# Loads of w_in for two chunks at once, an order of their own for the weight loads, and a shifted attention of batch 1

One core of one Trainium2 chip. The metric is the device time of the whole kernel in microseconds (us), lower is better.

## The reference

```python
# 8 batches, 8 heads, 576 rows, 64 columns a head; 4608 tokens, 512 model columns, 2048 hidden columns
kv = np.einsum('bhsd,bhse->bhde', k, v)
out = np.einsum('bhsd,bhde->bhse', q, kv)
rms = np.sqrt(np.mean(out * out, axis=-1, keepdims=True) + 1e-06)
attn_out = (out / rms * g_norm).astype(np.float32)
x = attn_out.transpose(0, 2, 1, 3).reshape(B * S, H * D)
h = x @ w_in
g = np.maximum(0.01 * h, h)
return (g @ w_out).astype(np.float32)
```

The weights come in 64-bit floats. The kernel loads them as pairs of 32-bit words and rounds them to 32-bit floats on the chip.

## The kernel before

The tokens are worked off in nine blocks of 512. Blocks 1 to 8 are Strassen products on weights that are in SBUF. **Block 0** is the one that matters here. While it runs, 16 chunks of w_in and 16 of w_out are loaded and rounded, and in the gaps the attention of batch 1 is computed for block 1. It has 16 steps. Step n computes `h_ps` (8 matmul records), ScalarE makes `gT` of it, and one step later `o_acc` takes `gT` and a rounded chunk of w_out.

One rounding **job** is two ScalarE and four VectorE instructions. Jobs are numbered 0 to 31 in the order in which they are rounded.

```python
def round_f64(dst, raw):
    ...
    pin(nc.scalar.activation(add, lo, func=AF.Copy, scale=2.0 ** -29))
    pin(nc.scalar.activation(cut, hi.bitcast(F32), func=AF.Copy, scale=2.0 ** -112))
    pin(nc.vector.tensor_scalar(cut, cut, HIGH_MOST, -HIGH_MOST, op0=ALU.min, op1=ALU.max))
    pin(nc.vector.tensor_scalar(dst, cut, 3, None, op0=ALU.logical_shift_left))
    pin(nc.vector.scalar_tensor_tensor(dst, in0=cut, scalar=0x80000000, in1=dst,
                                       op0=ALU.bitwise_and, op1=ALU.bitwise_or))
    pin(nc.vector.tensor_tensor(dst, dst, add, op=ALU.add))
# ... (cut)
def first_block(between):
    for n in range(2 * NC * U + 1):                 # 17 turns, 16 steps
        now = last
        if n < 2 * NC * U:
            # ... the matmuls into h_ps, eight records (cut)
            nc.scalar.activation(gT, h_ps, func=AF.Prelu, alpha=SLOPE)      # not pinned
            last = (gT, w2_sb[h][c][:, u, :], n)
        # ...
        between(n, 0)
        # ... the matmuls into o_acc, eight records (cut)
        between(n, 1)
# ... (cut)
steps.update((i, a1) for a1 in [attention(1)]
             for i in (12, 13, 15, 16, 18, 20, 21, 23, 24, 26, 27, 28))
def between(n, half):
    go(steps.get(2 * n + half, iter(())), 1)        # one piece of the attention
    while half and rounded < min(3 * n + 8, 2 * n + 13, len(w_jobs)):
        if loaded < len(w_jobs):
            load_w(loaded)                          # into seven buffers in turn
            loaded += 1
            if loaded in (15, 19):
                load_pair(1, (loaded - 15) // 4)    # k, v and q of two heads of batch 1
        round_w(rounded)
        rounded += 1
```

What is in `pin(...)` keeps the program's order among the pinned instructions of its engine; what is not pinned is placed by a scheduler, by its own model of when data is ready.

Of the kernel before, what the change touches and what calls it, by code (L numbers as in the profile page):

```python
# [22 lines left out]
def kernel(  # L23
# [50 lines left out]
    stage = ctx.enter_context(tc.tile_pool(name="stage", bufs=3))  # L74
# [3 lines left out]
    wcomb = ctx.enter_context(tc.tile_pool(name="wcomb", bufs=1))  # L78
    gpool = ctx.enter_context(tc.tile_pool(name="gpool", bufs=2))
    opool = ctx.enter_context(tc.tile_pool(name="opool", bufs=2))  # L80
# [5 lines left out]
    def matmul(*args, **kw):  # L86
        pin(nc.tensor.matmul(*args, **kw))  # L87

# [30 lines left out]
    def load_first():  # L119

        early = xpool.tile([P, NE * NT], F32, tag="xT", name="early")
        n = J * D

        def rows(t):
# [5 lines left out]
        ks, vs = (t + [rows(wcomb.tile([P, 4 * U * P], F32, tag=f"pair{i + j}",  # L130
                                       name="early_kv")) for i in range(2)]
# [27 lines left out]
    raw_homes = itertools.cycle([(stage, "raw")] * 3 + [(wcomb, f"pair{i}") for i in range(4)])  # L159

    def load(t, src):

        if len(src.shape) == len(t.shape):
            t, src = [t], [src]
        else:
            n = src.shape[1]
            t = [t[i * n:(i + 1) * n] for i in range(src.shape[0])]
        for to, part in zip(t, src):
            pin(nc.sync.dma_start(to, part))

    def load_f64(src):
        a, n = src.shape[-2:]
        n //= 2
        pool, tag = next(raw_homes)
        raw = pool.tile([P, a * n, 2], U32, tag=tag, name="raw")
        load(raw.rearrange("p (a n) two -> p a (n two)", a=a), src)
        return raw

    def round_f64(dst, raw):
# [10 lines left out]
        lo, hi = raw[:, :, 0], raw[:, :, 1]  # L190
        add = spare(a * n, "add", U32)
        pin(nc.scalar.activation(add, lo, func=AF.Copy, scale=2.0 ** -29))
        cut = spare(a * n, "cut")
# [3 lines left out]
        add, cut = (t.rearrange("p (a n) -> p a n", a=a) for t in (add, cut.bitcast(U32)))  # L197
# [6 lines left out]
    w_jobs = []  # L204
    for c in range(NC):
        for h in range(2):
            for u in range(U):
                f0 = h * (DF // 2) + (c * U + u) * P
                w_jobs += [(w1_sb[h][c][:, u], w_in_e[:, :, :, f0:f0 + P]),
                           (w2_sb[h][c][:, u:u + 1, :], w_out[f0:f0 + P].unsqueeze(1))]  # L210

    w_jobs[1:-1] = [w_jobs[i + 1 if i % 2 else i - 1] for i in range(1, len(w_jobs) - 1)]
    w_raws = {}

    def load_w(j):
        dst, src = w_jobs[j]
        if w_in.dtype == I64:
            w_raws[j] = load_f64(src.bitcast(U32))
        else:
            load(dst, src)  # L220

    def round_w(j):
        if w_in.dtype == I64:
            round_f64(w_jobs[j][0], w_raws.pop(j))
# [97 lines left out]
    def attention(b):  # L322
# [10 lines left out]
        for m in range(2):  # L333
            turn(2 * m)
            yield
            turn(2 * m + 1)
            if m:
                yield
            attention_kv(b, m, kv_ps)
            for p in (2, 3) if m == 0 else (0, 1):  # L340
                if b + m < B:
                    load_pair(b + m, p)
            yield
# [5 lines left out]
    def first_attention():  # L349
# [12 lines left out]
        for j in range(3):  # L362
            load_w(j)
# [13 lines left out]
        for i in range(2):  # L377
            nc.vector.tensor_copy(
                qT.rearrange("p a (t j) -> p a t j", j=J)[:, i::2, :, J - 1], rest[i])
        for m in range(2):  # L380
# [4 lines left out]
        for j in range(3, 7):  # L385
            load_w(j)
# [13 lines left out]
        for j in range(1, 5):  # L400
            round_w(j)

# [4 lines left out]
    def sides_w1(c):  # L407
# [4 lines left out]
        s12 = wcomb.tile([P, 2, U, 2, P], F32, tag="pair0", name="ws")  # L412
        sides = {1: a11, 2: a12, 4: a22, 5: s12[:, 0], 6: s12[:, 1]}
# [3 lines left out]
        def more():  # L417
            s34 = wcomb.tile([P, 2, U, 2, P], F32, tag="pair1", name="ws")
# [246 lines left out]
```

## Time and profile before

| | before |
|---|---|
| time, median of 3 runs | 976.85 us (976.59 to 978.72) |
| TensorE busy | 954.6 us of a span of 974.5 (98%) |
| VectorE, ScalarE, GpSimd busy | 430.2, 270.1, 507.9 us |
| first rounding job starts on ScalarE | 18.11 us |
| first o_acc group starts | 37.89 us |
| first product of block 1 (h_a) starts | 157.51 us |

### The profile page before, as it was taken

The page shows a single profiled execution, that of the slowest core. Times are in us where ns is not written, and L with a number is a line of the kernel's source. Part 1 is how long each engine was busy: PE and PEld are TensorE (multiplying, and loading weights), DVE is VectorE, ACT ScalarE, POOL GpSimd, SP SyncE. Part 2 cuts the span into 40 slices and gives each one's busy share as a digit, 9 for nine tenths or more (in the row PEclk, how much of TensorE's full clock was granted, in tenths as well). Part 3 has the DMA queues.
Part 4 walks back from the last instruction along what each step waited for, and adds up shares of the span by engine and source line. Part 5 has one row for each costly group of instructions (what it writes and reads, how often), then busy time and mean ns, then how long its engine had stood idle before and what let it go on. Part 6 is the DMA issues. An engine that isn't in the chain of part 4 may idle for free.

```text
span 974.5 us, 14053 instructions
## 1 busy us (share of the span) xinstructions
PE 954.6 (98%) x5702; PEld 762.3 (78%) x5702; DVE 430.2 (44%) x688; ACT 270.1 (28%) x531; POOL 507.9 (52%) x399
## 2 busy tenths in 40 slices
PE   8899998999999999999999999999999999999997
PEld 4444345888888888888888888888888888888886
DVE  3966873256224543256224832373235422431223
ACT  3634531232123311332123212331223121112210
POOL 1000203556655565666665665566565766666664
PEclk9899998999999999999999999999999999999999
DMA  9989702500152004300430044002200000001001
GB/s 248 215 217 252 197 1 84 153 1 1 40 149 50 1 11 130 97 1 1 141 97 1 1 126 111 1 1 65 77 1 1 11 33 1 1 12 33 1 0 44
DMA packets 36161, 63.48 MB, mean 65 GB/s; under 512 B 4864, under 2 KB 21248, under 8 KB 36096
## 3 DMA queue, kind: packets, MB, share of 16 engines
q1 hardware_dynamic: 26112, 51.95, 20.8%
q10 hardware_dynamic: 9856, 10.62, 3.2%
q8 instruction: 45, 0.74, 0.3%
q14 instruction: 20, 0.16, 0.1%
q0 software_dynamic: 128, 0.00, 0.0%
HBM read 53.12 MB, written 9.44 MB: 64 GB/s over the span
## 4 chain that ended last, share of the span: by engine, by line
PE 94%; DVE 2%; DMA 2%; ACT 1%; issue 0%; SPq 0%; ACTq 0%
PE h_a L87 23%; PE o_a L87 23%; PE h_c L87 17%; PE o_c L87 17%; PE h_ps L87 5%; PE o_acc L87 5%; PE o_ps L87 2%; DMA k_in<-in_k_dram 2%; PE kv_ps L87 2%; DMA raw<-in_moe_w_in_dram 1%; DVE w L199 0%; DVE w L201 0%; ACT cut L194 0%; DVE qT L329 0%; DVE xT L309 0%
## 5 line engine op out<-in xcount | busy, mean ns | idle before, releaser
L405 POOL TENSOR_TENSOR ws<-w 128x512 f32<-128x512 f32 x33 | 46.4, 1407 | 288.6 <-PE h_c L87 247.7
L405 DVE TENSOR_TENSOR o<-o_a,o 128x512 f32<-128x512 f32 x104 | 71.6, 688 | 203.3 <-PE o_a L87 203.2
L484 ACT ACTIVATE g<-g 128x512 f32<-128x512 f32 x96 | 60.5, 630 | 292.5 <-DVE g L405 292.5
L405 POOL TENSOR_TENSOR ws<-w,w 128x512 f32<-128x512 f32 x33 | 43.5, 1318 | 150.5 <-ACT cut L194 101.4
L87 PE MATMUL o_a<-wt,gs 128*128 128x256 f32 x512 | 120.9, 379 | 0.0
L87 PEld LDWEIGHTS o_a<-wt,gs 128*128 128x128 f32 x512 | 97.3, 190 | 13.2
L405 DVE TENSOR_TENSOR o<-o_c,o 128x512 f32<-128x512 f32 x88 | 60.5, 687 | 89.5 <-PE o_c L87 89.5
L405 POOL TENSOR_TENSOR wt<-w,wt 128x512 f32<-128x512 f32 x64 | 83.2, 1300 | 2.5
L405 POOL TENSOR_TENSOR gs<-g,g 128x512 f32<-128x512 f32 x64 | 83.2, 1323 | 0.3 <-ACT g L484 0.2
L405 DVE TENSOR_TENSOR g<-h_c,g 128x512 f32<-128x512 f32 x64 | 44.0, 688 | 85.6 <-PE h_c L87 85.6
L87 PE MATMUL h_ps<-xT,w 128*128 128x512 f32 (+1 forms) x136 | 60.2, 588 | 6.9 <-DVE xT L309 6.1
L87 PE MATMUL o_acc<-w,gT 128*128 128x512 f32 x128 | 60.7, 619 | 3.7 <-DVE w L201 3.7
L87 PE MATMUL h_a<-xT,w 128*128 128x256 f32 x256 | 61.2, 382 | 0.7 <-ACT g L484 0.7
L87 PE MATMUL o_a<-w,g 128*128 128x256 f32 x256 | 60.6, 379 | 0.8 <-DVE o L405 0.8
L87 PE MATMUL h_a<-xt,w 128*128 128x256 f32 x256 | 61.1, 382 | 0.0
L87 PE MATMUL h_c<-xT,w 128*128 128x256 f32 x256 | 61.1, 381 | 0.0
L87 PE MATMUL h_a<-xt,ws 128*128 128x256 f32 x256 | 61.1, 381 | 0.0
L87 PE MATMUL h_a<-xT,ws 128*128 128x256 f32 x256 | 61.1, 381 | 0.0
L87 PE MATMUL h_c<-xt,ws 128*128 128x256 f32 x256 | 61.1, 381 | 0.0
L87 PE MATMUL o_c<-wt,gs 128*128 128x256 f32 x256 | 60.5, 379 | 0.0
L87 PE MATMUL h_c<-xT,ws 128*128 128x256 f32 x256 | 60.5, 379 | 0.0
L87 PE MATMUL o_a<-wt,g 128*128 128x256 f32 x256 | 60.5, 379 | 0.0
(84 smaller groups left out, 1607.6 us busy)
## 6 DMA issues: line engine op xcount, KB each, us to landing
out_dram<-o ACTq DMA_DIRECT2D x36, 256.0 KB, 2.2
v_in<-in_v_dram SPq DMA_DIRECT2D x30, 288.0 KB, 4.9
raw<-in_moe_w_in_dram SPq DMA_DIRECT2D x64, 128.0 KB, 5.8
raw<-in_moe_w_out_dram SPq DMA_DIRECT2D x16, 512.0 KB, 6.8
k_in<-in_k_dram SPq DMA_DIRECT2D x28, 288.0 KB, 4.2
q_in<-in_q_dram SPq DMA_DIRECT2D x56, 144.0 KB, 4.5
q_in<-in_q_dram SPq DMA_DIRECT2D x56, 140.0 KB, 4.5
k_in<-in_k_dram ACTq DMA_DIRECT2D x2, 288.0 KB, 9.2
```

The costliest lines, as they stand in the source:

```text
L87: pin(nc.tensor.matmul(*args, **kw))
L405: eng.tensor_tensor(out_, a, b_, op=ALU.subtract if minus else ALU.add)
L484: nc.scalar.activation(t, t if src is None else src, func=AF.Prelu, alpha=SLOPE)
```

## The change

The intent is to load the weights faster and sooner. Two neighbouring chunks of w_in share one read, in runs of 2 KB instead of 1 KB (all but the first two chunks, which keep runs of 1 KB). The loads run ahead in an order of their own, limited only by three buffers each for w_in and w_out. The last w_out chunks no longer queue behind batch 2, whose loads now stand after block 0 in the program. The attention of batch 1 is moved to where its data should be there.

```diff
+    stage = consts.tile([P, 6 * U * 2 * P], F32, name="stage")
+    early = xpool.tile([P, NE * NT], F32, tag="xT", name="early")
+    raw_in = itertools.cycle((stage[:, :2 * RAW], early, flat(ws_place)))
+    raw_out = itertools.cycle((stage[:, 2 * RAW:], flat(wt_place)[:, :RAW],
+                               flat(wt_place)[:, RAW:]))
...
+    def loads_w():
+        for h, c, u in chunks:
+            if u == 0:
+                ... (stop here until the job that used the buffer has been rounded)
+                n = P if (h, c) == (0, 0) else U * P
+                for i in range(0, U * P, n):
+                    load_words(raw[:, :, words * i:words * (i + n)],
+                               w_in_w[:, :, :, words * (f0 + i):words * (f0 + i + n)])
+                    yield True
+            ... (the same for one chunk of w_out)
...
-                if b + m < B:
+                if 1 < b + m < B and b > 1:
                     load_pair(b + m, p)
...
-    steps.update((i, a1) for a1 in [attention(1)]
-                 for i in (12, 13, 15, 16, 18, 20, 21, 23, 24, 26, 27, 28))
-    loaded, rounded = 7, 5
+    a1 = attention(1)
+    steps.update((i, a1) for i in (12, 14, 20, 21, 22, 23, 24, 26, 27, 28, 29, 30))
+    rounded = 5
...
+        if (n, half) == (8, 0):
+            load_pair(1, 2)
+            load_pair(1, 3)
         while half and rounded < min(3 * n + 8, 2 * n + 13, len(w_jobs)):
-            ... (one load for each job)
             round_w(rounded)
             rounded += 1
+            load_ahead()
+            if rounded in (12, 16):
+                load_pair(1, (rounded - 12) // 4)
     first_block(between)
+    go(a1)
+    for p in range(2):
+        load_pair(2, p)
```

More of the change, by code (lines that the diff above doesn't have):

```diff
@@ L73 @@
     consts = ctx.enter_context(tc.tile_pool(name="consts", bufs=1))
-    stage = ctx.enter_context(tc.tile_pool(name="stage", bufs=3))
     ins = ctx.enter_context(tc.tile_pool(name="ins", bufs=2))
@@ L77 @@
     xpool = ctx.enter_context(tc.tile_pool(name="xpool", bufs=3))
-    wcomb = ctx.enter_context(tc.tile_pool(name="wcomb", bufs=1))
     gpool = ctx.enter_context(tc.tile_pool(name="gpool", bufs=2))
-    opool = ctx.enter_context(tc.tile_pool(name="opool", bufs=2))
     ps_att = ctx.enter_context(tc.tile_pool(name="ps_att", bufs=2, space=bass.MemoryType.PSUM))
@@ L87, in matmul @@
         pin(nc.tensor.matmul(*args, **kw))
+    ws_place = consts.tile([P, 4, U * 2 * P], F32, name="ws")
+    wt_place = consts.tile([P, 4, U * N2], F32, name="wt")
+    o_place = consts.tile([P, 6, 2 * N2], F32, name="o")
+    stage = consts.tile([P, 6 * U * 2 * P], F32, name="stage")
+    early = xpool.tile([P, NE * NT], F32, tag="xT", name="early")
     k_ins, v_ins, q_ins = {}, {}, {}
@@ L119, in load_first @@
     def load_first():
-        early = xpool.tile([P, NE * NT], F32, tag="xT", name="early")
+        o_flat = o_place.rearrange("p a n -> p (a n)")
         n = J * D
@@ L129, in load_first @@
         qs += [rows(early[:, i * n:]) for i in range(2)]
-        ks, vs = (t + [rows(wcomb.tile([P, 4 * U * P], F32, tag=f"pair{i + j}",
-                                       name="early_kv")) for i in range(2)]
+        ks, vs = (t + [rows(o_flat[:, (i + j) * n:]) for i in range(2)]
                   for j, t in ((0, ks), (2, vs)))
@@ L157, in spare, with flat @@
         return gpool.tile([P, n], dtype, tag=next(spare_homes), name=name)
-    raw_homes = itertools.cycle([(stage, "raw")] * 3 + [(wcomb, f"pair{i}") for i in range(4)])
-    def load(t, src):
-        if len(src.shape) == len(t.shape):
-            t, src = [t], [src]
-        else:
-            n = src.shape[1]
-            t = [t[i * n:(i + 1) * n] for i in range(src.shape[0])]
-        for to, part in zip(t, src):
-            pin(nc.sync.dma_start(to, part))
-    def load_f64(src):
-        a, n = src.shape[-2:]
-        n //= 2
-        pool, tag = next(raw_homes)
-        raw = pool.tile([P, a * n, 2], U32, tag=tag, name="raw")
-        load(raw.rearrange("p (a n) two -> p a (n two)", a=a), src)
-        return raw
+    def flat(t):
+        return t.rearrange("p a n -> p (a n)")
+    RAW = 2 * NE * P
+    raw_in = itertools.cycle((stage[:, :2 * RAW], early, flat(ws_place)))
+    raw_out = itertools.cycle((stage[:, 2 * RAW:], flat(wt_place)[:, :RAW],
+                               flat(wt_place)[:, RAW:]))
     def round_f64(dst, raw):
         a, n = dst.shape[1:]
-        lo, hi = raw[:, :, 0], raw[:, :, 1]
-        add = spare(a * n, "add", U32)
+        lo, hi = raw[:, :, :, 0], raw[:, :, :, 1]
+        add = spare(a * n, "add", U32).rearrange("p (a n) -> p a n", a=a)
         pin(nc.scalar.activation(add, lo, func=AF.Copy, scale=2.0 ** -29))
-        cut = spare(a * n, "cut")
+        cut = spare(a * n, "cut").rearrange("p (a n) -> p a n", a=a)
         pin(nc.scalar.activation(cut, hi.bitcast(F32), func=AF.Copy, scale=2.0 ** -112))
@@ L196, in round_f64 @@
         dst = dst.bitcast(U32)
-        add, cut = (t.rearrange("p (a n) -> p a n", a=a) for t in (add, cut.bitcast(U32)))
+        cut = cut.bitcast(U32)
         pin(nc.vector.tensor_scalar(dst, cut, 3, None, op0=ALU.logical_shift_left))
@@ L203 @@
     w_in_e = w_in.rearrange("(p t i) f -> p i t f", p=NP, i=E)
-    w_jobs = []
-    for c in range(NC):
-        for h in range(2):
-            for u in range(U):
-                f0 = h * (DF // 2) + (c * U + u) * P
-                w_jobs += [(w1_sb[h][c][:, u], w_in_e[:, :, :, f0:f0 + P]),
-                           (w2_sb[h][c][:, u:u + 1, :], w_out[f0:f0 + P].unsqueeze(1))]
+    chunks = [(h, c, u) for c in range(NC) for h in range(2) for u in range(U)]
+    w_jobs = [(w, *at) for at in chunks for w in (1, 2)]
@@ L212, with load_words @@
     w_jobs[1:-1] = [w_jobs[i + 1 if i % 2 else i - 1] for i in range(1, len(w_jobs) - 1)]
     w_raws = {}
-    def load_w(j):
-        dst, src = w_jobs[j]
+    def load_words(t, src):
+        parts = [src] if len(src.shape) == len(t.shape) else [src[i] for i in range(src.shape[0])]
+        n = P // len(parts)
+        for i, part in enumerate(parts):
+            pin(nc.sync.dma_start(t[i * n:(i + 1) * n], part))
+    def loads_w():
+        words = 2 if w_in.dtype == I64 else 1
+        w_in_w, w_out_w = ((w_in_e.bitcast(U32), w_out.bitcast(U32)) if words == 2
+                           else (w_in_e, w_out))
+        of_in, of_out = [], []
+        for h, c, u in chunks:
+            f0 = h * (DF // 2) + (c * U + u) * P
+            if u == 0:
+                of_in.append([(1, h, c, v) for v in range(U)])
+                if len(of_in) > 3:
+                    while any(job not in rounded_w for job in of_in[-4]):
+                        yield False
+                raw = next(raw_in)[:, :words * NE * U * P]
+                if words == 2:
+                    raw = raw.bitcast(U32)
+                raw = raw.rearrange("p (t f) -> p t f", t=NE)
+                n = P if (h, c) == (0, 0) else U * P
[3 more added lines that the diff above has]
+                    yield True
+                for v in range(U):
+                    w_raws[1, h, c, v] = raw[:, :, words * v * P:words * (v + 1) * P]
+            of_out.append((2, h, c, u))
+            if len(of_out) > 3:
+                while of_out[-4] not in rounded_w:
+                    yield False
+            raw = next(raw_out)[:, :words * DM]
+            if words == 2:
+                raw = raw.bitcast(U32)
+            load_words(raw, w_out_w[f0:f0 + P])
+            w_raws[2, h, c, u] = raw.rearrange("p (t f) -> p t f", t=1)
+            yield True
@@ L217, in load_w, with load_ahead, round_w @@
+    rounded_w = set()
+    w_loads = loads_w()
+    def load_ahead():
+        for done in w_loads:
+            if not done:
+                return
+    def round_w(j):
+        job = w, h, c, u = w_jobs[j]
+        dst = w1_sb[h][c][:, u] if w == 1 else w2_sb[h][c][:, u:u + 1, :]
+        raw = w_raws.pop(job)
         if w_in.dtype == I64:
-            w_raws[j] = load_f64(src.bitcast(U32))
+            round_f64(dst, raw.rearrange("p a (n two) -> p a n two", two=2))
         else:
-            load(dst, src)
@@ L222, in round_w @@
-    def round_w(j):
-        if w_in.dtype == I64:
-            round_f64(w_jobs[j][0], w_raws.pop(j))
+            nc.vector.tensor_copy(dst, raw)
+        rounded_w.add(job)
     eps_sb = consts.tile([P, 1], F32, name="eps_sb")
@@ L361, in first_attention @@
         rest = [ps_m.tile([P, NP // 2, 64], F32, tag=t, name="rest_ps") for t in ("oc", "oa")]
-        for j in range(3):
-            load_w(j)
         for p in range(NP):
@@ L384, in first_attention @@
         copy_kv(0, kv_ps)
-        for j in range(3, 7):
-            load_w(j)
         round_w(0)
@@ L401, in first_attention @@
             round_w(j)
+            load_ahead()
     def add(eng, out_, a, b_, minus=False):
@@ L411, in sides_w1 @@
         a21, a22 = w1_sb[1][c][:, :, :2, :], w1_sb[1][c][:, :, 2:, :]
-        s12 = wcomb.tile([P, 2, U, 2, P], F32, tag="pair0", name="ws")
-        sides = {1: a11, 2: a12, 4: a22, 5: s12[:, 0], 6: s12[:, 1]}
+        s = [ws_place[:, i].rearrange("p (u e m) -> p u e m", u=U, e=2) for i in range(4)]
+        sides = {1: a11, 2: a12, 4: a22, 5: s[0], 6: s[1], 7: s[2], 3: s[3]}
         add(nc.gpsimd, sides[5], a21, a22)
@@ L417, in more @@
         def more():
-            s34 = wcomb.tile([P, 2, U, 2, P], F32, tag="pair1", name="ws")
-            sides.update({7: s34[:, 0], 3: s34[:, 1]})
             add(nc.gpsimd, sides[7], a11, a21, True)
@@ L428, in sides_w2 @@
         b21, b22 = w2_sb[1][c][:, :, :N2], w2_sb[1][c][:, :, N2:]
-        t12 = wcomb.tile([P, 2, U, N2], F32, tag="pair2", name="wt")
-        sides = {1: b11, 2: b21, 3: b22, 5: t12[:, 0], 6: t12[:, 1]}
+        t = [wt_place[:, i].rearrange("p (u m) -> p u m", u=U) for i in range(4)]
+        sides = {1: b11, 2: b21, 3: b22, 5: t[0], 6: t[1], 7: t[2], 4: t[3]}
         add(nc.gpsimd, sides[5], b12, b11, True)
@@ L434, in more @@
         def more():
-            t34 = wcomb.tile([P, 2, U, N2], F32, tag="pair3", name="wt")
-            sides.update({7: t34[:, 0], 4: t34[:, 1]})
             add(nc.gpsimd, sides[7], b22, b12, True)
@@ L511, in product_h @@
                             lambda i, part, r: x_sides[i][:, r, :], done)
+    o_places = itertools.cycle(range(6))
     def product_o(c, w_sides, g_sides, os, finish):
@@ L515, in product_o @@
             for key in ("11", "12", "21", "22"):
-                os[key] = opool.tile([P, 2, N2], F32, tag="o", name=f"o{key}", bufs=6)
+                os[key] = o_place[:, next(o_places)].rearrange("p (t m) -> p t m", t=2)
         into = {1: ("11", True), 5: ("22", True), 2: ("11", False), 6: ("12", True),
@@ L574, in first_block @@
         for t in range(4):
-            o = opool.tile([P, DM], F32, tag="o", name="o", bufs=6)
+            o = o_place[:, next(o_places)]
             if t % 2:
@@ L583 @@
     steps = {i: tail for tail in [tail_of(0, NT, S)] for i in (6, 8, 10)}
-    steps.update((i, a1) for a1 in [attention(1)]
-                 for i in (12, 13, 15, 16, 18, 20, 21, 23, 24, 26, 27, 28))
-    loaded, rounded = 7, 5
+    a1 = attention(1)
+    steps.update((i, a1) for i in (12, 14, 20, 21, 22, 23, 24, 26, 27, 28, 29, 30))
+    rounded = 5
     def between(n, half):
-        nonlocal loaded, rounded
+        nonlocal rounded
         go(steps.get(2 * n + half, iter(())), 1)
+        if (n, half) == (8, 0):
+            load_pair(1, 2)
+            load_pair(1, 3)
         while half and rounded < min(3 * n + 8, 2 * n + 13, len(w_jobs)):
-            if loaded < len(w_jobs):
-                load_w(loaded)
-                loaded += 1
-                if loaded in (15, 19):
-                    load_pair(1, (loaded - 15) // 4)
             round_w(rounded)
             rounded += 1
+            load_ahead()
+            if rounded in (12, 16):
+                load_pair(1, (rounded - 12) // 4)
     first_block(between)
+    go(a1)
+    for p in range(2):
+        load_pair(2, p)
     x_sides, more_x = sides_x(xTs.pop(1))
```

## The prediction

> **What bounds the kernel now.** I read the page first (busy shares, then the 40 slices), then the waits, then the chain of work that ended last, then the timeline around each gap of TensorE. The page's slices:
>
> ```profile
> PE   8899998999999999999999999999999999999997
> PEclk9899998999999999999999999999999999999999
> DMA  9989702500152004300430044002200000001001
> GB/s 248 215 217 252 197 1 84 153 1 1 40 149 50 1 11 130 97 1 1 141 97 1 1 126 111 1 1 65 77 1 1 11 33 1 1 12 33 1 0 44
> ```
>
> A slice is 24.4 us. TensorE is full from slice 7 on; the change can only win in slices 0 to 6 (block 0, where the weights are loaded and rounded while the matmuls already run). The first five slices are also the only ones in which the DMA engines are full. So I looked for the waits of TensorE in them, in the table of waits of TensorE:
>
> ```profile
> PE h_ps L87 <- DVE xT L309: 6.1, 2, 4.9
> PE o_acc L87 <- DVE w L201: 3.7, 1, 3.7
> PE o_ps L87 <- DVE kv L260: 2.1, 2, 1.6
> ```
>
> The first lies before 34.35 us, in the start that the change leaves alone. The other two are the matter. The chain shows what they cost:
>
> ```profile
> 100.58 6.64 DMA k_in<-in_k_dram
> 107.22 1.23 DVE qT L329
> 108.44 0.31 DVE kv L260 x2
> 108.76 1.17 DVE qT L329
> 109.92 0.04 issue
> 109.97 0.94 PE o_ps L87 x4
> 110.91 3.63 PE h_ps L87 x8
> ...
> 144.80 0.66 ACT add L192
> 145.46 0.56 ACT cut L194
> 146.04 0.44 DVE cut L195
> 146.50 1.38 DVE w L198
> 147.91 1.64 DVE w L199
> 149.57 1.65 DVE w L201
> 151.36 6.32 PE o_acc L87 x8
> 157.68 1.73 PE h_a L87 x8
> ```
>
> Gap one: the o_acc group before it ended near 106.9 and o_ps takes 0.91 when nothing holds it (the later one at 117.97), so it could have ended at 107.8; it ended at 110.9. 3.1 us lost. Gap two: the last chunk of w_out is rounded only after the last gT, TensorE idles 3.65 us, and the next eight records take 6.32 us instead of 3.43: 6.5 us lost. Together **9.6 us is all there is to win**: 976.85 - 9.6 = 967.3, 1.0%. A gain over 2% would need 19.5 us, which no gap of block 0 holds.
>
> **What the Trainium skill says.** "TensorE: Matmul & The Clock Gate", What's actually happening: after an idle window of about 3.4 us the array's clock is halved, until a busy window has passed. The trace agrees: after the 3.65 us gap the records take 0.79 us each instead of 0.43, and the granted clock of 140 to 160 us is 0.83; the 1.7 us gap at 107 cost no clock. "GPSIMD Engine Reference", Key points: GpSimd shares its SBUF interfaces with VectorE. The trace agrees: between 146.5 and 151.2 us three rounding steps beside GpSimd adds take 1.37, 1.63 and 1.64 us, where they take 0.43, 0.69 and 0.69 alone. That is about 0.95 us of VectorE lost per GpSimd add; the transposes beside GpSimd at 107 us keep their 1.25. "DMA: Bandwidth & Descriptors", Specifications: 512 B is enough for line rate. Here the trace's packet records of 20 to 60 us differ a little: 1 KB reads (w_in) take 82 ns in the mean, 4 KB reads (mostly w_out) 278 ns, so w_in moves at about 0.85 of the rate per byte of w_out.
>
> **The change part by part.** (1) *2 KB runs.* 14 of the 16 w_in chunks come in runs of 2 KB. From the two packet means a 2 KB packet would take some 145 ns (estimate, straight line), so per chunk of 0.52 MB, spread over 16 engines, 0.3 us is saved, 4 us in all; if the line is steeper, as the bursts of 330 to 380 GB/s in narrow windows with w_out suggest, up to 16 us. None of it is on TensorE's path by itself, it only lets data land earlier. (2) *Order of loads.* Weights run as far ahead as three buffers each for w_in pairs and w_out allow, the last w_out no longer waits behind 2.3 MB of batch 2, and the last two pairs of batch 1 come behind all weights. In the built program's order of instructions the last rounding now stands on ScalarE before gT of step 12 instead of behind gT of step 15. **Gap two goes: -6.5 us.** (3) *Attention of batch 1.* On TensorE the first kv group moves from before h of step 7 to behind it, the second from behind h of step 9 to behind h of step 11, and the first o_ps (448 columns) from behind o_acc of step 9 to behind h of step 12. On VectorE the last two transposes of q, which that o_ps needs, now stand behind rounding job 30 of 0 to 31; before, behind job 24 or so. That is where I expect the gain to go.
>
> The walk on TensorE without any wait: o_acc of step 5 ends at 76.8 as now, h of step 7 at 80.2. Then kv 1.2, o_acc 3.6, and h, o_acc, h, o_acc, h, o_acc, h at 3.43 each: h of step 11 ends at 109.1; kv 1.2, o_acc 3.6, h 3.4: step 12's o_ps could start at 117.3. Behind it stand eight groups and three small o_ps, 29.9 us. Block 1 could start at 117.3 + 0.9 + 29.9 = 148.1 instead of 157.7: the 9.6 us again.
>
> The walk on VectorE: on ScalarE job 15 now stands behind gT of step 7 (in the kernel before job 15 started at 73.9, behind gT of step 6). Step 7's h ends at 80.2, gT takes 0.6, add and cut 1.2: VectorE starts job 15 at 82.1, and idles before that for some 8 us. From there to the o_ps it has jobs 15 to 30, 16 x 2.25 us (start to start of the cut rows at 97.1, 99.4, 101.6, 103.9) = 36.0, four transposes of q at 1.2 = 4.8, the kv copies 0.3: 123.2 at the best. Beside it GpSimd does four ws adds (freed by job 21) and four wt adds (freed by jobs 28 and 30), 8 x 0.95 = 7.6, less one that falls on a transpose: 7. So **the last transpose ends near 130 us, 12 us after TensorE could use it.** The last o_ps records 0.9, then 29.9: 161.0. An idle time of 10 us halves the clock; priced as the measured 2.9: 163.9. Against 157.7 that is +6.2: 983. If GpSimd costs VectorE nothing: 123.2 + 0.9 + 29.9 + 2.9 = 156.9, -0.8: 976.
>
> Everything behind block 1's start I leave as it is: TensorE is idle for under 1 us of 300 to 960, and the batch 2 loads (now from about 115 us) have 40 us until they are needed.
>
> **The rivals.** (a) *The gain arrives.* The data was the limit, all of it lands early, and rounding keeps up: 967 to 970. For it: DMA full for 110 us, gap one started with a wait for q. Against: the VectorE walk, which needs 16 jobs in the 35 us between 82 and 117. It would hold if the rounding of jobs 15 on is not held behind gT of step 7. (b) *VectorE's rounding becomes the bound*, as worked out: 976 to 986. (c) *k and v of the last pair land late.* Jobs 16, 18, 20, 22, 24 and 26 free the buffers of the last six w_out chunks, so the load queue stalls with them: the last w_out would go out at about 107 and pair 3's k and v, 1.8 MB behind it at some 290 GB/s (the rate while batch 1 loads, 80 to 85 us, was 298), 6 us, plus 1.5 to land, at about 115 to 116, while TensorE wants them at 109 to 111. That is a wait of 5 us at the kv group, but it lies inside the wait of (b) and adds little, except a second half-clock stretch (up to +3): 979 to 989. If (b) is smaller than I think, (c) alone makes 971 to 975.
>
> **Range and chances.** (b) with GpSimd's share gets about 60%, (a) 25%, (c) the rest, drawn toward (a) because a schedule called "moved to fit" was probably tried out. That makes 980, with 967 to 988 for 8 in 10. Over 2% faster would be under 957, below the 9.6 us limit: 1%. Over 2% slower would be over 996, 14 us above the walk's result: 3%.
>
> **What would show each step right or wrong.** Right: no wait of o_acc for w at the end of block 0 and the last wt and ws adds well before it; the waits of TensorE headed by o_ps behind h of step 12, released by VectorE's qT; VectorE without a gap from about 82 to 130 us; the last q transpose at 127 to 132; GpSimd adds beside slow rounding steps; the DMA engines with idle gaps near 62 to 66, 78 to 83 and 100 to 107 us. The prediction is wrong if block 1's first h_a starts near 148 (then (a)), if ScalarE starts job 15 before 78 us, or if the wait sits at kv with a DMA as releaser and the o_ps does not wait (then (c)).

## More of the kernel before

The prediction shows the slices, the waits of TensorE and the chain. One view that it did not use is needed later, ScalarE's timeline at the start (start, duration, engine, line, operation, output from input, shape, and in brackets the idle time before it with what ended it):

```profile
18.11 0.66 ACT L192 ACTIVATE add<-raw 128x512 uint32<-128x512 uint32 x1 [3.82 <-DMA raw<-in_moe_w_in_dram]
```

The first rounding waits for the first chunk of w_in: four transfers.

## The result, and the profile after

After: **981.66 us** median (981.22 to 982.05, 4 runs). Before, beside it: 977.41 (976.59 to 978.72, 4 runs). Ratio 1.0042, 95% interval 1.0025 to 1.0059: within 2%, and slower by about 4 us. Here and below a ratio is the mean time of one kernel's fast runs over that of the other's of the same rounds, so it isn't quite the ratio of the medians quoted.

The page's slices of the changed kernel:

```profile
PE   8799699999999999999999999999999999999997
...
DMA  8687731510043004300430034001200000001001
```

Slices 0 to 4 had the DMA engines at 9, 9, 8, 9, 7 before; now they are at 8, 6, 8, 7, 7. The loads were meant to come sooner, and the DMA engines are idle more. TensorE has lost the dent in slice 6 (146 to 171 us) and has got one in slice 4 (98 to 122 us). The two longest waits of TensorE from 15 to 175 us (line, what it waited for: us in all, times, longest):

```profile
PE kv_ps L84 <- DMA v_in<-in_v_dram: 6.8, 2, 4.3
PE h_ps L84 <- DVE xT L349: 6.4, 2, 5.2
```

The wait of o_acc for w at the end of block 0 (3.7 us) is gone, and so is its half-clock stretch. In its place kv waits 6.8 us for v of the last two pairs (2.45 and 4.35 us). The chain of work that ended last:

```profile
113.52 7.42 DMA v_in<-in_v_dram
120.94 0.14 issue
121.08 2.19 PE kv_ps L84 x70
123.27 5.44 PE o_acc L84 x8
128.72 3.43 PE h_ps L84 x8
132.15 1.17 PE o_ps L84 x16
...
156.38 6.87 PE o_acc L84 x16
163.25 1.73 PE h_a L84 x8
```

The kv and o_acc records behind the wait take 2.19 and 5.44 us where they take 1.21 and 3.63 at full clock. Block 1 starts 5.6 us later than before. VectorE's timeline tells of the other limit:

```profile
85.30 0.43 DVE L188 TENSOR_SCALAR cut<-cut 128x512 f32<-128x512 f32 x1 [9.63 <-ACT cut L187]
...
129.60 1.25 DVE L369 STREAM_TRANSPOSE qT<-q_in 128x576 f32<-128x576 f32 x1
130.70 0.47 DVE L300 COPY kv<-kv_ps 128x128 f32<-128x128 f32 x2
131.09 1.23 DVE L369 STREAM_TRANSPOSE qT<-q_in 128x576 f32<-128x576 f32 x1
```

VectorE idles 9.6 us until ScalarE starts job 15 at 84.03, right behind gT of step 7 (83.53):

```profile
83.53 0.60 ACT L602 ACTIVATE gT<-h_ps 128x512 f32<-128x512 f32 x1 [6.27 <-PE h_ps L84]
84.03 0.67 ACT L185 ACTIVATE add<-early 128x512 uint32<-128x512 uint32 x1
```

From there it works without a gap until the last transpose of q ends at 132.3. The o_ps group needs that transpose, and it starts at 132.15 on the chain: the chain names the late v, but **both paths end together at 132**.

The load queue stands behind the same jobs. Waits of SyncE's queue, 15 to 150 us, of the kernel before:

```profile
SPq L169 <- ACT cut L194: 6.4, 7, 1.3
```

and of the changed kernel:

```profile
SPq L208 <- ACT cut L187: 58.8, 12, 13.6
```

A weight load waits until ScalarE's `cut` of an old job has read its buffer: 6.4 us before, 58.8 us now. Last, ScalarE's timeline at the start:

```profile
20.43 0.67 ACT L185 ACTIVATE add<-stage 128x512 uint32<-128x512 uint32 x1 [5.73 <-DMA stage<-in_moe_w_out_dram]
```

The first rounding is 2.3 us later. The first two chunks of w_in now lie interleaved in one stretch of `stage`, and the instruction waits for eight transfers instead of four: in the landing records of the trace the eighth read of w_in ends at 20.20, right before it. (The line names w_out, but that transfer ended at 21.32, when the rounding was under way. The transfers take eight semaphores in turn, which may be why the view names another.) ScalarE works in order (the Trainium skill, "PSUM — Partial Sum Buffer", Engine vs sequencer instructions, calls its queue strict FIFO; the trace agrees, since the first attention's `sum` comes at 21.55 right behind this job instead of at 19.58). The first o_acc starts at 41.19 instead of 37.89.

### The profile page after: what moved, and what is told of

Its sections match the earlier page's. It is cut to its first block, busy times and chain, and to the rows that moved or that the text cites. A ratio compares the mean times of both kernels' runs of the same rounds, so it can differ in the third digit from the quotient of the medians.

```text
span 980.3 us, 13995 instructions
## 1 busy us (share of the span) xinstructions
PE 956.2 (98%) x5702; PEld 764.7 (78%) x5702; DVE 434.1 (44%) x688; ACT 270.1 (28%) x531; POOL 507.2 (52%) x399
## 4 chain that ended last, share of the span: by engine, by line
PE 87%; DVE 3%; DMA 1%; issue 0%; SPq 0%; ACT 0%; DVEq 0%
PE h_a L84 23%; PE o_a L84 23%; PE h_c L84 17%; PE o_c L84 17%; PE o_acc L84 2%; PE o_ps L84 2%; PE kv_ps L84 2%; PE h_ps L84 1%; DMA v_in<-in_v_dram 1%; DVE w L192 1%; DVE w L194 1%; DVE cut L188 0%; DVE w L191 0%; DVE qT L369 0%; SPq L121 0%
## 5 line engine op out<-in xcount | busy, mean ns | idle before, releaser
L444 POOL TENSOR_TENSOR gs<-g,g 128x512 f32<-128x512 f32 x64 | 82.1, 1304 | 0.6
L84 PE MATMUL o_c<-w,gs 128*128 128x256 f32 x256 | 60.5, 379 | 0.0
L84 PE MATMUL o_c<-w,g 128*128 128x256 f32 x256 | 60.5, 379 | 0.0
```

Source lines behind the costliest of these rows:

```text
L84: pin(nc.tensor.matmul(*args, **kw))
L444: eng.tensor_tensor(out_, a, b_, op=ALU.subtract if minus else ALU.add)
```

## The experiments

The edits stand against the changed kernel unless it is said otherwise. All were run with five rounds; runs e1 to e4, e5 to e8 and e9 to e12 each shared a chip and the runs of the kernel before (medians 977.33, 977.84, 977.31). "kv" is the start of the second kv group of batch 1 with all its data, "o_ps" that of the first 448-column o_ps group with all of its; these are starts in the timelines, which lie about 0.1 us ahead of the chain's.

| run | time, us | ratio to before (95%) | job 0 | first o_acc | kv | o_ps | block 1 |
|---|---|---|---|---|---|---|---|
| before | 977.41 | | 18.11 | 37.89 | 95.26 | 109.97 | 157.51 |
| after | 981.66 | 1.0042 (1.0025 to 1.0059) | 20.43 | 41.19 | 121.08 | 132.08 | 163.08 |
| e1 first chunks apart | 979.33 | 1.0025 (1.0010 to 1.0040) | 18.07 | 38.44 | 117.48 | 128.63 | 160.34 |
| e2 gT pinned | 976.81 | 0.9997 (0.9980 to 1.0015) | 20.96 | 41.61 | 120.12 | 128.39 | 159.14 |
| e3 pinned, further ahead | 978.67 | 1.0017 (1.0002 to 1.0032) | 21.02 | 41.20 | 121.73 | 130.00 | 160.75 |
| e4 = e1 + e2 | 975.21 | 0.9982 (0.9967 to 0.9997) | 19.18 | 39.06 | 117.22 | 125.49 | 156.24 |
| **e5 = e1 + pinned from step 6** | **967.53** | **0.9898 (0.9885 to 0.9911)** | 18.79 | 38.68 | 109.79 | 118.06 | 148.81 |
| e6 no k, v loads | 982.84 | 1.0058 (1.0046 to 1.0070) | 20.98 | 40.73 | 113.45 | 130.82 | 164.20 |
| e7 no k, v loads, q at hand | 971.04 | 0.9932 (0.9920 to 0.9944) | 20.58 | 40.76 | 113.48 | 121.75 | 152.50 |
| e8 less VectorE work | 978.62 | 1.0011 (0.9996 to 1.0026) | 20.72 | 40.48 | 115.56 | 126.54 | 157.29 |
| e9 pinned from step 6 alone | 969.58 | 0.9920 (0.9907 to 0.9933) | 20.31 | 40.04 | 111.15 | 119.42 | 150.17 |
| e10 w_in in 1 KB runs | 982.10 | 1.0046 (1.0033 to 1.0060) | 20.49 | 40.86 | 120.14 | 131.25 | 162.75 |
| e11 GpSimd's sums later | 976.12 | 0.9990 (0.9971 to 1.0008) | 21.03 | 40.77 | 117.34 | 127.69 | 158.43 |
| e12 before, pinned from step 6 | 976.81 | 0.9989 (0.9973 to 1.0004) | 18.89 | 39.74 | 97.11 | 108.82 | 158.08 |

**The theory** after the two traces: the time went into two places. The start lost 2 to 3 us to the coupled first chunks. In block 0, the scheduler's place for job 15, behind gT of step 7 on ScalarE, held back the rounding, and with it VectorE's last transposes and the load queue. **The rivals**: the transfers themselves limit (late k and v by themselves, or the runs of w_in); the start is swallowed by the later waits.

### e1: the first two chunks in stretches of their own

```diff
-                for i in range(0, U * P, n):
-                    load_words(raw[:, :, words * i:words * (i + n)], ...)
+                m = words * NE * n
+                halves = [raw[:, i * m:(i + 1) * m].rearrange("p (t f) -> p t f", t=NE)
+                          for i in range(U * P // n)]
+                for i, half in enumerate(halves):
+                    load_words(half, ...)
 ... (the rounding then takes each half; cut)
```

> Only edit against the changed kernel: the first two chunks of w_in are loaded each into a stretch of SBUF of its own, so the first rounding waits for 4 transfers instead of 8. Theory S (the missed 3.3 us of the start come from this coupling and travel to the end): the first rounding on ScalarE starts near 18.1 us instead of 20.4, the half-clock stretch behind it is about 7 us long instead of 13.7, the first o_acc is back near 38 us from 41.2, and the whole is 2 to 3.5 us under the changed kernel (981.7), at 978 to 980. Rival S2 (later waits, set by the load queue and VectorE, swallow what the start wins): the start moves but the time stays within 1 us of 981.7. Rival S3 (the start was late for another cause, the two kernels' memory layout or transfer rate): the first rounding stays near 20 us.

ScalarE's timeline of this run:

```profile
18.07 0.68 ACT L185 ACTIVATE add<-stage 128x512 uint32<-128x512 uint32 x1 [3.35 <-DMA stage<-in_moe_w_in_dram]
```

The first rounding is back at 18.1, the first o_acc at 38.44, and block 1 starts 2.7 us earlier. The time is 979.33, 2.3 us under the changed kernel. The two intervals overlap, so the times alone don't settle it; the trace shows the shift from end to end, and e9 against e5 repeats it. Over all traces, job 0 starts at 20.3 to 21.0 us in the nine kernels with the shared tile and at 18.1 to 19.2 us in the five without it, 2.1 us apart in the mean. One thing was not as expected: the half-clock stretch did not shrink to 7 us (the granted clock of 24 to 38 us was 0.63, against 0.52 after). From the first h_ps to the first o_acc the kernels took 11.3 to 12.3 us: 12.3 in the changed kernel, but 11.3 in e6, e8, e9 and e11, which have the same start. So of the 3.3 us at the start, 2.3 are the coupling; the other 1.0 I put down to the phase of the clock, which no run isolates. "TensorE: Matmul & The Clock Gate" of the Trainium skill, What's actually happening, says that the window is free-running and the count of slow matmuls varies from run to run; these starts agree.

### e2, e3, e4: gT in program order

```diff
-                nc.scalar.activation(gT, h_ps, func=AF.Prelu, alpha=SLOPE)
+                pin(nc.scalar.activation(gT, h_ps, func=AF.Prelu, alpha=SLOPE))
...
-        while half and rounded < min(3 * n + 8, 2 * n + 13, len(w_jobs)):
+        while half and rounded < min(3 * n + 8, 2 * n + 9, len(w_jobs)):
```

e3 has `2 * n + 11` there. e4 is this edit together with that of e1.

> Only edit against the changed kernel: ScalarE's gT are kept in program order between the rounding jobs, with the rounding 4 jobs less ahead in the program, so that job 15 follows gT of step 4 instead of gT of step 7 and two jobs stand between each pair of gT. Theory O (the order on ScalarE holds back rounding, and with it the release of the w_out buffers, the load queue and the last transposes of q): the gap of VectorE before job 15 (9.6 us in the changed kernel) is gone, wait of kv for v_in (6.8 us) goes under 2 us, o_ps (1.8 us) under 1 us; 971 to 975. Rival R (the rate of the transfers limits: all data simply arrives no earlier): the wait of kv stays at 4 us or more and the time within 2 us of 981.7. In its instruction order the loads of pairs 2 and 3 also stand ahead of the last two w_out loads, so a wait of o_acc for the last w_out could come back (up to 6 us).

> As the run before, with the rounding one step further ahead: job 17 follows gT of step 4. Theory O: like the run before or up to 2 us better, since the last w_out jobs come one step earlier; 970 to 975. If rounding so far ahead makes gT wait behind rounding whose data is not there[...], the h or o_acc groups of steps 4 to 8 wait for gT instead, and it is slower than the run before by what that wait shows. Rival R: within 2 us of 981.7.

> Both edits: first chunks apart, and gT pinned with the rounding 4 jobs less ahead. If the two causes are separate and add up, its time is that of the pinned kernel less 2 to 3.5 us: 968 to 972, which would be 6 to 9 us under the kernel before. If the start's gain is swallowed by later waits, it equals the pinned kernel within 1 us.

In all three, the waits of kv for v_in and of o_ps for q are gone, as the theory of the order asked; no wait for the last w_out came back. The times are only half of what it asked, because a new wait is there, here in the waits of e4:

```profile
PE o_acc L84 <- ACT gT L603: 5.3, 1, 5.3
```

The pin put gT of step 3 behind two rounding jobs and ScalarE's work for the last rows of batch 0 (`sq`, `spread`), which itself waits for an o_ps group that TensorE does one h later, at 60.2. TensorE idled 5.27 us and its next group took 5.41 instead of the usual 3.60 in this view. e2 has the same wait (5.3 us), e3 one of 6.4 us. The order theory is supported by what went away, but these runs alone do not show the whole of the gain. e4 is 1.6 us under e2.

The smaller constant moves more than gT. It puts rounding jobs later in the program, and whatever stands between them earlier by comparison. In e2 and e4 VectorE's last two transposes of q come behind jobs 26 and 27 instead of 30, and k and v of the last two pairs go out ahead of the last two w_out chunks instead of behind them (in e3: behind job 28, and ahead of the last w_out alone). So the edit has three parts, the order on ScalarE, on VectorE and in the load queue. e5 and e9 take it over, and no run has the pin or the constant by itself.

### e5: both edits, gT pinned from step 6 on only

```diff
-                nc.scalar.activation(gT, h_ps, func=AF.Prelu, alpha=SLOPE)
+                g = nc.scalar.activation(gT, h_ps, func=AF.Prelu, alpha=SLOPE)
+                if n >= 6:
+                    pin(g)
```

with `2 * n + 9` and the edit of e1.

> As the kernel with both edits (975.2), but gT are pinned from step 6 on only, so the gT of the early steps stay where the scheduler had them in the changed kernel; four rounding jobs stand between gT of steps 5 and 6, two between each pair after it. In the kernel with both edits the wait that was left was one of o_acc for gT of step 3 (5.3 us at 60 to 66 us, with a half-clock stretch behind it), because the pin put that gT behind rounding jobs and the tail of block 1's first rows. Theory: that wait goes and no other comes, block 1 starts at 149 to 151 us instead of 156.4, and the time is 968 to 971. Rival: the rounding and the loads behind it then come too late for a TensorE that is 7 us earlier, and the wait of kv for v_in or of o_ps for q returns: 972 to 976.

967.53 us, 10 us under the kernel before (ratio 0.9898) and 14 under the changed kernel, with a correct result. Behind the start no wait over 1 us is left up to 175 us:

```profile
PE h_ps L84 <- DVE xT L350: 6.8, 2, 5.2
```

Jobs 15 to 18 now stand between gT of steps 5 and 6: job 15 starts at 67.9 instead of 84.0, right behind gT of step 5:

```profile
67.38 0.57 ACT L603 ACTIVATE gT<-h_ps 128x512 f32<-128x512 f32 x1
67.86 0.67 ACT L185 ACTIVATE add<-early 128x512 uint32<-128x512 uint32 x1
```

The load queue's waits for ScalarE's `cut` fall from 58.8 to 32.6 us, and the DMA share of 84 to 110 us is 0.93 instead of 0.69. Block 1 starts at 148.81; the prediction's walk without waits had 148.1. **This version beats both kernels.** Beside the edit of e1 it takes three lines for the pin and a constant.

### e6, e7: are the late k, v and the late transposes two waits side by side?

Both give a wrong result. e6 leaves out the loads of k and v of pairs 2 and 3 of batch 1 and reads the tiles of pairs 0 and 1 again. e7 does the same, and the last two transposes of q read the finished x of block 0.

```diff
+        if b == 1 and p > 1:
+            k_ins[b, p], v_ins[b, p] = k_old[p - 2], v_old[p - 2]
+        else: ... (load as before; keep pairs 0 and 1 in k_old, v_old)
...
             q_in = q_ins.pop((b, p))
+            if b == 1 and p > 1:                # e7 only
+                q_in = kept["x"].rearrange("p e n -> p (e n)")[:, :T * D]
```

> Wrong result on purpose. Against the changed kernel only the loads of k and v of pairs 2 and 3 of batch 1 are left out, and the kv group reads the tiles of pairs 0 and 1 again. If the two waits (kv for v_in, 6.8 us, and o_ps for the last transpose of q behind VectorE's rounding) stand side by side and end together at 132, as the trace of the changed kernel looks, taking the data alone away changes nothing: o_ps waits for VectorE instead, with 8 to 10 us of idle time of its own, and the time is within 1.5 us of 981.7. If the late k and v are the cause by themselves, kv no longer waits, o_ps waits under 2 us, and the time is 973 to 976.

> Wrong result on purpose. As the run before, and the last two transposes of q of batch 1 read data that is there (x of block 0), so that they stand early on VectorE and o_ps waits for neither. Rounding is unchanged. If the two waits cost the same time side by side, this one wins what neither wins alone: block 1 starts at 153 to 155 us instead of 163.3, the time is 971 to 974. If something else holds o_ps or block 1 (rounding of the last w_out, the kv copies behind VectorE's jobs), the time stays above 976 and the chain names it.

TensorE's timeline of e6, then of e7:

```profile
113.45 1.28 PE L84 MATMUL kv_ps<-v_in,k_in 64*64 64x64 f32 x72
130.82 2.79 PE L84 MATMUL o_ps<-qT,kv 64*32 64x448 f32 x8 [8.14 <-DVE qT L375]
```

```profile
113.48 1.28 PE L84 MATMUL kv_ps<-v_in,k_in 64*64 64x64 f32 x72
121.75 0.98 PE L84 MATMUL o_ps<-qT,kv 64*32 64x448 f32 x16
```

With k and v at hand, kv starts 7.6 us earlier and nothing is won: o_ps waits 8.14 us for the transpose instead, and the time is 982.84. With both gone the time is 971.04, 10.6 under the changed kernel. So the late data, alone, costs nothing: the wait that the changed kernel's table of waits shows first, with 6.8 us, is worth nothing by itself (the time is 1.2 us longer without it). Whether the transposes alone are worth nothing in the same way was not run by itself; e11 bears on it.

### e8: less work for VectorE

Jobs 15 to 31 leave out `scalar_tensor_tensor`. Its output is wrong, which doesn't matter for the time.

> Wrong result on purpose. Against the changed kernel jobs 15 to 31 leave out one of their four VectorE instructions (0.69 us alone, 1.65 beside GpSimd); ScalarE, the order and the loads are unchanged. 16 jobs before the last transpose of q give 11 to 13 us. If VectorE's pace sets both the last transposes and, by way of the buffers that the jobs free, the late k and v, both waits shrink: kv waits under 3 us for v_in, o_ps under 1.5, the time is 972 to 976. If the transfers themselves are the limit, kv's wait stays at 5 us or more and the time within 2 us of 981.7, since only one of two waits side by side is gone.

Between the two theories: kv still waits 3.7 us for v_in, o_ps for no transpose; 978.62 us, outside the ranges of both. The last pair's v went out at 107.8 instead of 113.5, since the jobs that free the buffers are done sooner, but landed 7.7 us later, as in the changed kernel (7.4). So VectorE's pace sets when the queue moves on, and the transfer itself then takes as long as ever. Six runs spread from 976.2 to 979.7, so the size is rough.

### e9: the pin and the constant without the edit of e1

e5 without the edit of e1.

> Against the changed kernel only the order on ScalarE: gT pinned from step 6 on, rounding 4 jobs less ahead (the first chunks of w_in stay coupled). If the start (about 2.5 us) and the order are two separate terms, this kernel gives 970 to 971, 2 to 3.5 us above the one with both (967.5) and 10 to 12 us under the changed kernel. If the order's gain needs the earlier start, or the later loads have slack enough to swallow the late start, it is under 968.5 or over 973.

969.58 us, just under the 970 to 971 expected: 12 us under the changed kernel from the pin and the constant, and 2.05 above e5. That fits e1's 2.3 for the start, so the two terms add up.

The expectation calls this the order on ScalarE, but the edit has the three parts named under e2 to e4. Job 15 starts on VectorE at 74.43 instead of 85.30 (10.9 us earlier), and the last transpose of q at 116.22 instead of 131.09 (14.9 us), with three jobs fewer ahead of it. The last pair's v goes out at 99.51 instead of 113.52, now ahead of the last two w_out (104.27 and 104.71). **The 12 us belong to the three together**; what each is worth was not run.

### e10: 2 KB runs undone

```diff
-                n = P if (h, c) == (0, 0) else U * P
+                n = P
```

> Against the changed kernel only one part undone: w_in in runs of 1 KB, one chunk at a time, in the same buffers and the same order; the order of the instructions on ScalarE and VectorE is the same in the built program. If the 2 KB runs gain what their packets show (149 ns for 2 KB against 82 ns for 1 KB, so some 0.3 us a chunk) and VectorE and ScalarE hold the rounding anyway, the time is within 1.5 us of 981.7. If the rate of w_in limits, it is slower by 3 us or more. Since each half may be waited for by itself, it could also be up to 1 us faster.

982.10 us, and the same waits (kv 6.2 us for v_in). The packet records from 34 to 110 us: 1 KB packets take about 75 ns in the mean here, 2 KB packets about 150 ns in the changed kernel. That is the same rate per byte, about 218 GB/s over 16 engines. **The 2 KB runs bring nothing** here.

### e11: GpSimd's first sums moved away from the rounding

```diff
     def add(eng, out_, a, b_, minus=False):
-        eng.tensor_tensor(out_, a, b_, ...)
+        i = eng.tensor_tensor(out_, a, b_, ...)
+        if eng is nc.gpsimd:
+            pin(i)
...
+    mark = consts.tile([P, 1], F32, name="mark")
+    pin(nc.gpsimd.tensor_copy(mark, late["gT"][:, :1]))     # gT of step 13
     h_sides, more = sides_w1(0)
```

So that the sums stay behind `mark`, all of GpSimd's sums are pinned, to the end of the kernel.

> Against the changed kernel only GpSimd's first eight side sums wait for gT of step 13 (near 147 us) by one small copy ahead of them, so that none runs beside the rounding. The prediction priced them at 0.95 us of VectorE each, 7 in all, and the trace shows four ws sums at 94 to 100 and four wt sums at 117 to 123. If that price is right and VectorE's pace sets both waits, VectorE's last transpose of q ends 6 to 7 us earlier (125 to 126), kv's data is 3 to 4 us earlier (only the ws sums lie ahead of its loads), and the time falls by 3 to 5 us, to 977 to 979. If the sums cost nothing that matters, it stays within 1 us of 981.7. A wait of block 1's third product for ws would show as a wait of h_a for GpSimd.

In the changed kernel GpSimd's timeline has the first of four ws sums and the first of four wt sums here:

```profile
94.49 1.37 POOL L444 TENSOR_TENSOR ws<-w 128x512 f32<-128x512 f32 x1 [90.41 <-ACT cut L187]
116.93 1.29 POOL L444 TENSOR_TENSOR wt<-w 128x512 f32<-128x512 f32 x1 [16.58 <-ACT cut L187]
```

In this run the ws sums start at 136.6 and the wt sums behind them, and VectorE's last transpose is

```profile
124.21 1.23 DVE L369 STREAM_TRANSPOSE qT<-q_in 128x576 f32<-128x576 f32 x1
```

6.9 us earlier than in the changed kernel; 0.4 of that is an earlier start of job 15 (84.87 instead of 85.30). kv's data is 3.7 us earlier, block 1 starts 4.65 us earlier, and the time is 976.12 (974.6 to 979.5), 5.5 less. Now that the transposes are out of the way, what holds block 1 is kv at 117.34. So the late data is a limit of its own, once the other is gone.

### e12: the kernel before with the better order on ScalarE

The kernel before with the pin from step 6 and `2 * n + 9`, nothing else.

> The kernel before with none of the change, only gT pinned from step 6 on and the rounding 4 jobs less ahead. If the order on ScalarE alone was what the kernel before lacked (its last rounding started at 144.8 behind gT of step 15, not behind a transfer), gap two goes and the time is 970 to 973; the change of the loads is then not needed for most of the gain. If the order of the loads limits (the last three w_out behind 2.3 MB of batch 2, pairs 2 and 3 of batch 1 behind the rounding), a wait for these data takes its place: 975 to 980.

976.81 us. Inside the range of the second theory, but not for its reason: on TensorE no wait for data took the place of the old gaps, though ScalarE waited 10.06 us for a chunk of w_in (until 94.14). Both gaps are gone (o_ps starts at 108.82 at full clock, the last 16 o_acc records follow one another in 7.03 us), and a wait for gT is new:

```profile
PE o_acc L87 <- ACT gT L565: 5.2, 1, 5.2
```

It is the same kind of wait as in e4: gT behind ScalarE's work for finished rows and two rounding jobs, at 121 us, with a half-clock stretch behind it. This execution also began late: its first o_acc was at 39.74, 1.85 us behind the kernel before, and its block 1 only 0.57 behind. So **how much of the 967.5 the change of the loads is needed for stays open**; an order for the kernel before that avoids this wait was not tried.

## Why the prediction was right or wrong

- **The class and the range held** (980.0 predicted, 967 to 988; 981.66 measured), and the rival (b) was the right one: VectorE was a bound at the o_ps group. But two terms were off and cancelled, so that 163.9 predicted for the start of block 1 and 163.25 measured lie so close is luck in part.
- **Gap two goes**: right. The end of block 0 has no wait, o_acc x16 takes 6.87 us.
- **Job 15 behind gT of step 7**: right. Predicted start on VectorE 82.1, measured 85.30; all of the 3.2 us are the late start of the whole, since gT of step 7 ends at 84.1 instead of 80.8. e5 and e9 undo it and win 12 us, but together with the orders on VectorE and in the load queue (see e9); the share of this place by itself is not shown.
- **VectorE saturated to 130, GpSimd taking 7 us of it**: right. 85.30 to 132.3 without a gap. e11 took the sums away and the last transpose came 6.9 us earlier, some 6.5 of it by the sums. In the trace the slow steps end 0.28 or 0.55 us after the GpSimd sum beside them: the sum at 97.23 ends at 98.68 and the VectorE step from 97.59 ends at 99.23. That fits "SBUF — State Buffer" of the Trainium skill, SBUF: two separate sides, by which the loser of the shared ports waits for the other's whole instruction.
- **Rival (c), "a wait of 5 us at the kv group, but it lies inside the wait of (b) and adds little"**: right in kind. The wait is 6.8 us, because the last w_out went out at 105.9 and 109.9 and kv's data landed at 121 instead of 115 to 116. e6 shows that it adds nothing. By the prediction's own list of signs, a wait at kv with a DMA as releaser and none at o_ps would have proved it wrong and (c) right. That is what the trace of the changed kernel shows (6.8 us at kv; o_ps has no wait for qT in its table), but the sign was badly chosen: with the late data taken away (e6), o_ps waits 8.14 us for qT. The wait is however not inside (b) with room to spare: the two end within 0.2 us of each other, and e11 shows (c) taking over as soon as (b) is 7 us shorter.
- **Wrong: "The first lies before 34.35 us, in the start that the change leaves alone."** It does not. The diff puts the first two chunks of w_in into one interleaved tile, and the first rounding waits for both. That is 2.3 us on the only path of the start (e1), 2 us of the whole time (e9 against e5); the trace shows 3.3 with the clock's phase. The diff had it: `n = P if (h, c) == (0, 0)` splits the loads, but not the tile.
- **Wrong: the term of 2.9 us for a half-clock stretch behind o_ps.** The idle time of the changed kernel lies at kv, 11 us ahead of o_ps, and its half clock (kv 1.0 and o_acc 1.8 us too long) is spent while VectorE is still busy, so it costs nothing. In e6, where TensorE idles at o_ps itself, the term is there: from o_ps to block 1 it takes 33.4 us instead of 31.0, though half of the group had run before the wait. The missed start (3.3) and this surplus term (2.9) nearly cancel.
- **Wrong: 0.3 us saved per w_in chunk by 2 KB packets.** The 2 KB packet, foreseen at 145 ns, took about 150, but the right thing to compare is 1 KB in the same kernel, about 75 ns (e10): nothing saved. It cost the prediction nothing, because no weight of it was on the path.
- **Rival (a) at 967 to 970** was not what the change does, but the limit of 967.3 behind it was right: e5 reaches 967.5. It does what the prediction named as (a)'s condition, that job 15 isn't held behind gT of step 7, and more (the orders named under e9, the start).

## What to carry to other kernels

When one engine works in order, a change of buffers or loads is also a change of that engine's order, and the scheduler's choice there can cost more than the loads save: compare the order of the built program, and pin only the stretch that needs it, since pins too far forward make their own waits. An edit that moves one engine's order can move another's and the loads': list all of them before naming the one that won. The first wait in the table may be worth nothing when another path ends at the same moment; take away one, then both, before believing it. A buffer that is shared by two loads couples their readers: look for it at the very start, where nothing hides it.

## What the Trainium skill lacked or had wrong

- "DMA: Bandwidth & Descriptors", Specifications, gives 512 B as enough for line rate. Here size above that did nothing for w_in (about 75 ns for 1 KB, 150 ns for 2 KB, 218 GB/s over 16 engines), but the 4 KB packets of w_out took 206 ns in the mean (318 GB/s) from 34 to 110 us of the changed kernel, and 251 ns (261 GB/s) in the same stretch of the kernel before. The page has no rates of loads by the length of a run that would tell these apart; the cause was not tested.
- "TensorE: Matmul & The Clock Gate", HAM oscillation, has a figure for gaps in the middle of a kernel, 1.67 us at half clock behind each, but for bursts of about 2 us between the gaps; by the page's sum half of it, some 0.8 us, is lost (an estimate from that figure). Here, where the work behind the gap goes on, waits of 5.15 to 5.27 us cost a further 1.8 (e4) and 2.9 us (e12) in the group behind them, and the two of 2.45 and 4.35 us at kv a further 2.8 us (after).
- "GPSIMD Engine Reference", Key points, names the contention but no size, and no page has one for these steps. Eight GpSimd sums beside VectorE's rounding cost its last transpose some 6.5 us (e11), and a step of 0.43 or 0.69 us alone takes 1.4 to 1.65.
